# Whole-set loads of x, a later GpSimd subtraction and a spread seam in a fused set-attention and SwiGLU kernel

## The chip, the cores and the metric

The kernel runs on one NeuronCore of one Trainium2 chip. Five engines run side by side, each with its own queue of instructions in program order: PE (TensorE, matrix products; its weight loads are listed as PEld), DVE (VectorE), ACT (ScalarE), POOL (GpSimd) and SP (SyncE, which here issues nearly all DMAs). They meet only at semaphores. The metric is the device time of one execution in microseconds, as the median of several runs.

## The reference

Two blocks follow each other. The first is an induced set attention over x (4 batches of 12416 rows of 128 channels) with 32 inducing vectors; the second is a SwiGLU feed-forward network (FFN) with an RMS norm in front.

```python
def mab(q, kv):
    s = scale * (q @ kv.transpose(0, 2, 1))
    s = s - s.max(-1, keepdims=True)
    a = np.exp(s)
    a /= a.sum(-1, keepdims=True) + 1e-09
    return a @ kv
h = mab(I, x)          # 32 inducing rows look at 12416 rows of x
y = mab(x, h)          # every row of x looks at the 32 rows of h
...
rms = np.sqrt(np.mean(y * y, axis=-1, keepdims=True) + 1e-06)
yn = y / rms * rms_g
g = yn @ w_gate                     # 128 -> 1536
out = ((g / (1 + np.exp(-g))) * (yn @ w_val)) @ w_out    # 1536 -> 128
```

The second attention's row sum drops out under the RMS norm, so the kernel never divides by it. And since a row of y is a combination of 32 rows of h, the kernel multiplies h into w_gate and w_val once per batch, and the FFN's first products work on the 32 attention weights of a row instead of its 128 channels. The three weight matrices arrive as 64-bit floats and are turned into 32-bit ones on the chip.

## The kernel before

**Sets, units and slots.** A batch's 97 blocks of 128 rows are cut into 7 sets `s` (five of 16 blocks, one of 15, one of 2). For the FFN a set is cut into 4 quarters, the last one into 1: these are the 25 *units* `u` of a batch, of 512 rows as a rule. A unit passes through the 12 chunks `j` of d_ff, and one chunk of one unit is a *slot*; a batch has 300. A slot (`slot` in `ffn`) issues the gate product `g` on PE (L653), the silu on ACT (L661), then the output products that are due (`products`), the value product `v` on PE (L664), the product u = silu times v on DVE (L670), and at last `steps()`: everything that was planned for this slot. The first two units go through their slots in turns.

**The output product** of a chunk comes in two kinds. A plain one is one 32-bit product on PE (L603, `acc<-u,wo`, two rows in the profile) and is issued at the earliest two slots after its u. The *three-part* one (`three`, `project3`) replaces it by three cheaper PE products (L619, L621, and L603 in its form `acc<-xn,xn`). It needs, in the slot after its own, a copy on ACT (L640) and a subtraction on POOL (L641), and a slot later another copy on ACT (L645) and another subtraction on POOL (L646). The third PE product reads what L646 wrote.

**The order is written out in advance.** `schedule(b)` gives each attention step of a batch a slot number; the seams (below) have theirs in a table. Within `steps()` the waiting steps come first (the two halves of three-part products, a finished unit's output), then the plan, then the seams, then `gather`. A small planner (the loop that fills `ready`) walks over all slots with the costs of POOL's work, 1.25 us a slot, and chooses which chunks become three-part products and in which slot their PE products are due; `sub_max` counts 1.1 us in the slot where it is planned, a seam's `scale`, `apply` and `split` count 3.0, 1.2 and 1.4. It chooses 400 of the 1200 chunks.

**The prologue** (before the first slot) does the first batch's attention without cover. `load_rows` loads set after set of x on SP's queue: set 0 in three pieces, sets 1 and 5 in two, the others in one; set 6 goes in four small ones (L141). A weight chunk is fetched (`fetch_raw`) after set 2 and four more after set 6. For each set PE turns the blocks (`turn_x`, L322), ACT copies them out (L325), PE multiplies by the inducing vectors (`scores1`, L331) and DVE takes scores and maxima out (L335). `scores1` of a set comes after `turn_x` of the next one. DVE's work on the first weight chunk is put in between: `parts(0, 0)` (five instructions, L254 to L267 and L238) in the turn of set 3, `join(0, 0)` (L276, L282, then POOL's L284, a store and the next weight fetch) in that of set 4.

**Maxima.** `scores2(s)` writes the second attention's scores into the tile `sc` (L431); `sub_max(s)` takes each row's maximum on DVE (L436) and subtracts it on POOL (L437; for set 0 on DVE). Both are issued in one slot: in the first batch slot 2s+17, in the later ones, which are prepared under the batch before, slot 203+7s. ACT's exponential (`exp2`) follows from slot 30 and slot 254.

**Seams.** Between two sets, `seam(b, s)` makes the next set's FFN input in seven steps: `turn_a` (DVE, L499), `square` (PE, L505), `turn_z` (DVE, L512, L513), `scale` (DVE L517, L518, then a power on POOL, L520), `apply` (POOL, L524), `turn_b` (DVE, L528) and `split` (ACT L534, POOL L537). `gather` then brings a unit's rows together with four DMAs (L549); it is issued in chunk 2 of the unit before. The slots of the seven steps, counted from the first unit of the set before, stand in the line below: the first tuple for all seams but the first, the second for the first seam of batch 0.

```python
for i, step in enumerate(seam(*one)):
    j = ((14, 17, 18, 21, 21, 29, 31) if k else (32, 33, 33, 34, 34, 36, 38))[i]
    n, j = divmod(j, NJ)
    at = (b, firsts[s] + n + late_by, j)
```

## Time and profile before

| What | Value |
|---|---|
| median of 9 runs | 1673.86 us (1672.36 to 1675.46) |
| the profiled execution's own time | 1674.4 us |
| its span in the trace | 1672.6 us |
| mean granted TensorE clock | 0.998 |
| first FFN product (L653) starts at | 54.80 us |
| busy PE, ACT, DVE, POOL | 1654.5, 1237.0, 1175.5, 1160.3 us |
| DMA | 112.39 MB, mean 67 GB/s |

The 1200 slots take from 54.80 us to the end, 1.35 us each on the mean. Matmuls are pipelined and their ends are modelled: the idle time before a row, which the timeline gives in square brackets with what ended it, tells more than the busy time. A slot's place in time is found by its silu on ACT: the silus of slots 33, 38 and 48 start at 109.66, 116.00 and 132.77 us.

### The profile page before, as it was taken

The page shows a single profiled execution, that of the slowest core. Times are in us where ns is not written, and L with a number is a line of the kernel's source. Part 1 is how long each engine was busy: PE and PEld are TensorE (multiplying, and loading weights), DVE is VectorE, ACT ScalarE, POOL GpSimd, SP SyncE. Part 2 cuts the span into 40 slices and gives each one's busy share as a digit, 9 for nine tenths or more (in the row PEclk, how much of TensorE's full clock was granted, in tenths as well). Part 3 has the DMA queues.
Part 4 walks back from the last instruction along what each step waited for, and adds up shares of the span by engine and source line. Part 5 has one row for each costly group of instructions (what it writes and reads, how often), then busy time and mean ns, then how long its engine had stood idle before and what let it go on. Part 6 is the DMA issues. An engine that isn't in the chain of part 4 may idle for free.

```text
span 1672.6 us, 23254 instructions
## 1 busy us (share of the span) xinstructions
PE 1654.5 (99%) x6764; PEld 1036.4 (62%) x6764; DVE 1175.5 (70%) x1961; ACT 1237.0 (74%) x2234; POOL 1160.3 (69%) x931
## 2 busy tenths in 40 slices
PE   9999999999999999999999999999999999999998
PEld 6546566655676665665566666565567666666666
DVE  4878776676767877667677787667767666666665
ACT  4547778766787777776778777867677788788785
POOL 1337776767577775776578777577657888888884
PEclk9999999999999999999999999999999999999999
DMA  6445424343454131524345313252211111111111
GB/s 254 89 76 89 81 56 106 77 95 55 66 85 68 35 83 32 132 65 90 56 72 79 57 36 81 62 123 70 51 30 35 34 33 38 32 34 37 32 37 25
DMA packets 389743, 112.39 MB, mean 67 GB/s; under 512 B 365136, under 2 KB 369776, under 8 KB 387312
## 3 DMA queue, kind: packets, MB, share of 16 engines
q1 hardware_dynamic: 389424, 110.89, 32.6%
q8 instruction: 54, 0.88, 0.2%
q14 instruction: 73, 0.60, 0.1%
q10 hardware_dynamic: 192, 0.02, 0.0%
HBM read 53.95 MB, written 27.00 MB: 48 GB/s over the span
## 4 chain that ended last, share of the span: by engine, by line
PE 96%; DVE 1%; POOL 1%; DMA 1%; ACT 0%; issue 0%; SPq 0%; DVEq 0%; POOLq 0%
PE acc L603 45%; PE gv L653 17%; PE gv L664 16%; PE u L621 5%; PE u L619 5%; PE mm L331 3%; PE mm L505 1%; PE mm L384 1%; DMA xn<-in_x_dram 1%; DVE u L670 0%; POOL rs L520 0%; PE gv L322 0%; PE mm L457 0%; PE gv L331 0%; POOL xn L646 0%
## 5 line engine op out<-in xcount | busy, mean ns | idle before, releaser
L670 DVE TENSOR_TENSOR u<-silu,gv 128x512 f32<-128x512 f32 (+2 forms) x1186 | 779.8, 664 | 441.3 <-PE gv L664 227.5
L661 ACT ACTIVATE silu<-gv 128x512 f32<-128x512 f32 (+2 forms) x1186 | 691.8, 584 | 362.3 <-PE gv L653 326.8
L603 PE MATMUL acc<-u,wo 128*128 128x512 f32 (+2 forms) x1600 | 792.8, 579 | 1.2 <-DVE u L670 1.0
L664 PE MATMUL gv<-a,sv 128*128 128x512 f32 (+2 forms) x1188 | 759.8, 640 | 0.9 <-DVE u L670 0.9
L641 POOL TENSOR_TENSOR xn<-u,xn 128x512 fp32r<-128x512 f32 (+2 forms) x400 | 504.4, 1261 | 353.9 <-ACT xn L640 317.0
L646 POOL TENSOR_TENSOR xn<-hs,u 128x512 fp32r<-128x512 f32 (+2 forms) x400 | 504.4, 1261 | 39.6 <-ACT hs L645 36.6
L653 PE MATMUL gv<-a,sg 128*128 128x512 f32 (+2 forms) x1188 | 483.9, 407 | 0.0
L653 PEld LDWEIGHTS gv<-a,sg 128*128 128x128 f32 x1188 | 224.4, 189 | 228.9 <-ACT silu L661 110.9
L603 PEld LDWEIGHTS acc<-u,wo 128*128 128x128 f32 x1600 | 298.9, 189 | 77.9 <-issue 15.3
L664 PEld LDWEIGHTS gv<-a,sv 128*128 128x128 f32 x1188 | 224.3, 189 | 195.1 <-issue 135.9
L640 ACT ACTIVATE xn<-u 128x512 fp32r<-128x512 f32 (+2 forms) x400 | 247.7, 619 | 24.7 <-DVE u L670 22.8
L645 ACT ACTIVATE hs<-xn 128x512 f32<-128x512 f32 (+2 forms) x400 | 245.9, 615 | 5.6 <-POOL xn L646 4.2
L603 PE MATMUL acc<-xn,xn 128*128 128x512 f32 (+2 forms) x400 | 157.0, 392 | 4.5 <-POOL xn L646 4.5
L621 PE MATMUL u<-xn,xn 128*128 128x512 f32 (+2 forms) x400 | 155.6, 389 | 0.0
L619 PE MATMUL u<-xn,xn 128*128 128x512 f32 (+2 forms) x400 | 155.2, 388 | 0.0
L603 PEld LDWEIGHTS acc<-xn,xn 128*128 128x128 f32 x400 | 75.0, 188 | 25.1 <-POOL xn L646 8.6
L520 POOL TENSOR_TENSOR rs<-ms,mhalf 128x16 f32<-128x16 f32 (+2 forms) x28 | 75.9, 2711 | 16.5 <-DVE ms L518 14.7
L621 PEld LDWEIGHTS u<-xn,xn 128*128 128x128 f32 x400 | 75.1, 188 | 18.1
L619 PEld LDWEIGHTS u<-xn,xn 128*128 128x128 f32 x400 | 75.0, 188 | 16.9 <-issue 0.7
L612 DVE STREAM_TRANSPOSE o<-o 128x512 f32<-128x512 f32 (+2 forms) x97 | 67.7, 698 | 3.4
L611 DVE TENSOR_TENSOR o<-acc,o 128x512 f32<-128x512 f32 (+2 forms) x97 | 64.9, 669 | 0.0
L624 ACT ACTIVATE o<-u 128x512 f32<-128x512 f32 (+2 forms) x97 | 56.4, 582 | 0.0
(166 smaller groups left out, 774.0 us busy)
## 6 DMA issues: line engine op xcount, KB each, us to landing
out_dram<-o SPq DMA_DIRECT2D x320, 64.0 KB, 1.9
xn<-in_x_dram SPq DMA_DIRECT2D x62, 256.0 KB, 4.7
xT<-in_x_dram SPq DMA_DIRECT2D x60, 256.0 KB, 5.2
a<-hi SPq DMA_DIRECT2D x156, 64.0 KB, 2.0
a<-lo SPq DMA_DIRECT2D x156, 64.0 KB, 2.0
w<-w SPq DMA_DIRECT2D x22, 256.0 KB, 3.1
out_dram<-o SPq DMA_DIRECT2D x64, 60.0 KB, 1.9
xn<-in_x_dram SPq DMA_DIRECT2D x3, 1024.0 KB, 11.7
```

Of the source, the lines that this page charges most:

```text
L520: nc.gpsimd.tensor_tensor(out=rs, in0=ms, in1=mhalf[rows, 0:n], op=ALU.pow)
L603: nc.tensor.matmul(acc[:, 0:T], lhsT, rhs, start=st["left"] == NJ, stop=st["left"] == 1)
L619: nc.tensor.matmul(ups[:, 0:T], w[:, i, :], hi, start=st["k"] == nk, stop=False)
L621: nc.tensor.matmul(ups[:, 0:T], w[:, NK + i, :], lo, start=False, stop=not st["k"])
L640: nc.scalar.activation(hi, v, AF.Copy, scale=1.0 - 2.0 ** -13)
L641: nc.gpsimd.tensor_tensor(out=lo, in0=v, in1=hi.bitcast(F32), op=ALU.subtract)
L645: nc.scalar.activation(hs[:, 0:T], hi.bitcast(F32), AF.Copy, scale=1.0 + 2.0 ** -12)
L646: nc.gpsimd.tensor_tensor(out=d, in0=hs[:, 0:T], in1=v, op=ALU.subtract)
L653: nc.tensor.matmul(g[:, 0:T], sg[:, ts(j, P)], a[:, 0:T], start=True, stop=True)
L661: nc.scalar.activation(sl[:, 0:T], g[:, 0:T], AF.Silu)
L664: nc.tensor.matmul(v[:, 0:T], sv[:, ts(j, P)], a[:, 0:T], start=True, stop=True)
L670: nc.vector.tensor_tensor(out=t[:, 0:T], in0=sl[:, 0:T], in1=v[:, 0:T], op=ALU.mult)
```

## The change

There are three edits. x is loaded in whole sets but for set 0; with it the first `scores1` moves ahead of `turn_x(1)`, the first weight chunk is fetched after set 3 instead of set 2, and `parts` and `join` move one set later. `sub_max` is split: `row_max` (DVE) keeps the slot, the subtraction (POOL, or DVE for set 0) goes to the next one, and the planner counts it there. And in batch 0 the first seam's steps 2 to 6 go to slots 34, 35, 35, 39 and 41, with the gather behind them in chunk 6 of its unit instead of chunk 2. The lines that change:

```diff
-            for t0, t1 in (((0, R), (R, 2 * R), (2 * R, n)) if not s else ((0, 2 * R), (2 * R, n)) if s in (1, full - 1) else ((0, n),)):
+            for t0, t1 in (((0, R), (R, 2 * R), (2 * R, n)) if not s else ((0, n),)):
...
+        def row_max(s):
+            mx = st["mx2"] = small.tile([P, 16], F32, name="mx2")[rows2[s], 0:per2[s]]
+            nc.vector.reduce_max(out=mx, in_=weights(b, s), axis=AX.X)
+
         def sub_max(s):
-            n, v = per2[s], weights(b, s)
-            mx = small.tile([P, 16], F32, name="mx2")[rows2[s], 0:n]
-            nc.vector.reduce_max(out=mx, in_=v, axis=AX.X)
+            n, v, mx = per2[s], weights(b, s), st["mx2"]
             (nc.gpsimd if s else nc.vector).tensor_tensor(
...
-        for _ in range(1 if s == 2 else 4 if s == NS - 1 else 0):
+        for _ in range(1 if s == 3 else 4 if s == NS - 1 else 0):
...
-        if s:
-            f["scores1"](s - 1)
-        if s == 3:
+        if s != 1:
+            f["scores1"](max(s - 1, 0))
+        if s == 4:
             parts(0, 0, nc.vector)
-        if s == 4:
+        if s == 5:
             join(0, 0)
...
+    f["row_max"](0)
     f["sub_max"](0)
...
-                add(2 * s + 17, f["sub_max"], s)
+                add(2 * s + 17, f["row_max"], s)
+                add(2 * s + 18, f["sub_max"], s)
...
-                add(203 + 7 * s, g["sub_max"], s)
+                add(203 + 7 * s, g["row_max"], s)
+                add(204 + 7 * s, g["sub_max"], s)
...
-                j = ((14, 17, 18, 21, 21, 29, 31) if k else (32, 33, 33, 34, 34, 36, 38))[i]
+                j = ((14, 17, 18, 21, 21, 29, 31) if k else (32, 33, 34, 35, 35, 39, 41))[i]
...
-                if j == 2 and (b or u > 1) and (b, u) in after:
+                if j == (6 if (b, u) == (0, R - 1) else 2) and (b or u > 1) and (b, u) in after:
                     gather(*after[b, u])
```

## The prediction

> **What bounds the kernel now.** I read the page first. PE is busy nearly all the time and the chain that ended last runs through it:

> ```profile
> PE 1654.5 (99%) x6764; PEld 1036.4 (62%) x6764; DVE 1175.5 (70%) x1961; ACT 1237.0 (74%) x2234; POOL 1160.3 (69%) x931
> ...
> PE 96%; DVE 1%; POOL 1%; DMA 1%; ACT 0%; issue 0%; SPq 0%; DVEq 0%; POOLq 0%
> ```

> PE's work is the same after the change (1200 slots, 400 of them three-part), so only time in which PE waits or runs slowly can go. PE's waits come second:

> ```profile
> PE acc L603 <- POOL xn L646: 4.5, 4, 2.7
> ...
> PE mm L505 <- DVE eT L499: 0.6, 2, 0.4
> ```

> Behind the first slot POOL's L646 is the one releaser worth having: four waits, 4.5 us, one of 2.7. PE's timeline shows that one, in the first seam:

> ```profile
> 116.03 0.40 PE L621 MATMUL u<-xn,xn 128*128 128x512 f32 x1
> 119.12 0.74 PE L603 MATMUL acc<-xn,xn 128*128 128x512 f32 x1 [2.69 <-POOL xn L646]
> 119.65 0.63 PE L664 MATMUL gv<-a,sv 128*128 128x512 f32 x1
> ```

> The view by windows (PE's busy time comes second, the granted clock third from the end) adds that the clock drops right after:

> ```profile
> 116.50:119.20 2.70, 0.08 (x1) 0.09 (x1) 1.33 (x3) 1.17 (x3) 2.48 (x3) 1.00 0.00 0
> 119.20:122.70 3.50, 3.50 (x7) 2.09 (x8) 2.56 (x4) 0.63 (x2) 1.28 (x1) 0.51 0.21 53
> ```

> POOL's timeline tells why L646 is late: the power and the apply stand in front of it.

> ```profile
> 112.33 1.29 POOL L641 TENSOR_TENSOR xn<-u,xn 128x512 fp32r<-128x512 f32 x1 [7.81 <-ACT xn L640]
> 113.80 2.91 POOL L520 TENSOR_TENSOR rs<-ms,mhalf 128x16 f32<-128x16 f32 x1 [0.18 <-DVE ms L518]
> 116.78 1.05 POOL L524 TENSOR_TENSOR sc<-sc,rs 128x512 f32<-128x512 f32 x1
> 117.79 1.27 POOL L646 TENSOR_TENSOR xn<-hs,u 128x512 fp32r<-128x512 f32 x1
> ```

> The other three waits are one place, 405.7 us apart, where the subtraction L437 stands in front of L646 and itself waits 0.80 us for its maximum:

> ```profile
> 397.78 1.05 POOL L437 TENSOR_TENSOR sc<-sc,mx 128x512 f32<-128x512 f32 x1 [0.80 <-PE gv L653]
> 398.79 1.29 POOL L646 TENSOR_TENSOR xn<-hs,u 128x512 fp32r<-128x512 f32 x1
> ```

> Last the prologue, on DVE:

> ```profile
> 22.50 0.69 DVE L335 TENSOR_SCALAR_CACHE_REDUCE sc<-gv 128x512 f32<-128x512 f32 x1
> ...
> 23.72 0.69 DVE L282 SCALAR_TENSOR_TENSOR o<-sc,o 128x512 f32<-128x512 uint32 x1
> 25.29 0.69 DVE L335 TENSOR_SCALAR_CACHE_REDUCE sc<-gv 128x512 f32<-128x512 f32 x1 [0.88 <-PE gv L331]
> ...
> 26.60 0.66 DVE L335 TENSOR_SCALAR_CACHE_REDUCE sc<-gv 128x480 f32<-128x480 f32 x1 [0.61 <-PE gv L331]
> ```

> DVE has 0.88 and 0.61 us of slack there: that is what moved work can use up.

> **The first seam: -4.2 us.** With `scale` and `apply` a slot later, POOL's order becomes L641, L646, L520, L524: waiting steps come before seams. L641 ends at 113.62 and its copy L645 at 113.26, so L646 runs 113.6 to 114.9 instead of 117.79 to 119.07. PE has issued L621 at 116.03 and goes on at 116.27 (its rows lie 0.23 us apart elsewhere) instead of 119.12: 2.85 us. PE is then not idle, so the 3.41 us at half clock go too: half of them, 1.7 us. The window's sum is 4.55.

> What is late next? DVE: `turn_z` (L512, L513) moves behind slot 34's L670, `scale` behind slot 35's, so the power starts at about 115.1 instead of 113.80 and the apply ends at 119.15 instead of 117.84. `turn_b`, in slot 36, kept DVE idle for 2.74 us (L528 waiting for L524). In slot 39, with L670 (0.65 each) of slots 36 to 39, one L314 (0.69) and L611 and L612 (1.4) in front, DVE reaches it at about 119.65: no wait. In slots 39 to 43 DVE's L670 end just before PE wants them (slot 39's at 119.65, PE at 119.63); I allow 0.3 us for such waits, 0 to 1. The chunk of slot 38, newly three-part, is due in slot 44 (about 123.9); its L641 and L646 follow the apply and end at 121.8. -4.55 + 0.3 is about -4.2; bounds -4.6 (all of it) and 0 (another wait of the same size).

> The gather's four DMAs move on SP behind one xT load and unit 2's four stores, which go out earlier for it. L528 ends at 120.35, ACT's copy L534 is behind slot 41's silu (121.0), L537 waits for L646 and takes 1.28: 123.1. SP begins the stores when L612 is done, 119.3, and needs 3.37 us for them in this trace: 122.7; four issues of 0.6 bring the last to 124.5, and 2.0 from issue to landing (median of these DMAs) to 126.5. Unit 4's first product is wanted at 132.24 less 4.4, 127.8. Slack 1.3 us, cost 0; bounds 0 and, if they land as slowly as an xT load (5.2), 1.9.

> **The subtraction: -2.2 us.** In the first batch POOL has nothing between its six L437, so its order there, and the time, does not change; the exponential still stands behind the last. In later batches L646 of the preceding chunk now goes ahead of L437. At 397 it starts when L641 ends (396.98) and ends at 398.3; PE wants it at 399.36. The rows L621 to L603 lie 1.00 us apart there instead of 0.23: 0.77 in each of three places, 2.3; 0.1 is left for a later L641 behind the moved subtraction. The planner, by its own arithmetic, keeps its choice but for the chunk of slot 247, which becomes 245, in three batches. There the last subtraction (32x256, 0.61) does stand between L641 and L646. But its maximum is a slot old, so of 0.80 + 1.05 at the old place 0.61 are left: 1.24 less against a lateness of 0.77, so no wait. Bounds: -2.4, and 0 if each place only swaps one wait for another. Set 0's subtraction on DVE changes places with one L670, some 50 slots before its exponential: 0.

> **The prologue: +0.2 us.** DMA landings follow each other by bytes, 1 MB in 2.5 us (set 4's 18.97 after set 3's 16.47). The weight chunk (1.27 us) behind set 3 brings set 3 to 15.2, set 4 stays at 18.97, set 5 comes whole at 21.4 to 21.9. The three DMAs fewer save issue time that nothing waits for. `scores1(0)` needs ACT's fourth copy of set 0 (ends 10.12) and fills 10.15 to 11.2 while set 1 lands (10.0 to 10.2); `turn_x(1)` follows, then sets 2 (13.0) and 3 (15.9 instead of 16.61); set 4 waits for its load, 19.1 instead of 19.47. PE is 0.35 us ahead. DVE is not: L335 of set 3 at 22.1, `parts` 22.7 to 24.9 (2.14 in this trace), L335 of set 4 to 25.5, `join` (0.60 + 0.69) to 26.8, and only then L335 of set 5, 26.8 instead of 26.60. All that follows the maximum shifts by +0.2. `join`'s POOL product (1.27), its store and the fetch behind it come 2.4 us later: the weights are first used at 40.43, the fetched chunk at 58.39 (it landed at 30.81): 0. Bounds: -0.4 (PE's lead counts) and +1.0, as follows. In before PE turns blocks without a break from 7.58 to 11.4, and at 9.7 its rows begin to come at twice the pace. After the change it stands still from 9.4 to 10.15, and another 3.4 us at half pace (the one length this trace shows) would cost 1.7, of which the waits for loads hide 0.7.

> [...]

> **Sum.** -4.2 - 2.2 + 0.2 = -6.2 us. The profiled execution took 1674.4 (span 1672.6 and 1.8 around it) and becomes 1668.2; it lies 0.54 above the median, so the median becomes 1667.7, 0.37% less. About 0.2%, 3.3 us, is what a measurement of this kernel can tell from no change.

> **Rivals.**
> 1. *The seam's stall only moves* (7 in 100). PE waits as long elsewhere in slots 36 to 48, for u behind `turn_b` or for the gather. For it: DVE has no slack in slots 39 to 43. Against: no wait above 0.3 us comes out. -2.2 + 0.2 = -2.0: 1671.9, no measurable change.
> 2. *The subtractions only swap waits* (8 in 100). For it: slot 245 has the order that cost 0.77. Against: its maximum is there, and it is the short one. -4.2 + 0.2 = -4.0: 1669.9.
> 3. *The break in the prologue puts the full clock off* (10 in 100). -4.2 - 2.2 + 1.0 = -5.4: 1668.5.
> 4. *Slower* (5 in 100): in the three later batches L646 behind the moved subtraction comes so late that PE stands as in the first seam. Each such place costs 2.85 + 1.7 = 4.55 us; three make 13.7: 1674.4 - 4.2 + 0.2 + 13.7 - 0.5 = 1683.6. It turns the sign by 0.2% from 3.9 us a place on. Against: five slots (6.7 us) lie between chunk and product, and 0.63 + 1.29 + 0.61 + 1.29 = 3.8 must fit.

> **How the numbers follow.** The sum as worked has 70 in 100, its own range is 1666.0 to 1669.5 (the bounds -0.4 of the prologue and -4.6, -2.4 on one side, 1 us of DVE waits and 0.9 of a late gather on the other). Low 1665.8; high 1671.0 takes in rivals 2 and 3 and leaves out 1 and 4, 12 in 100, and some of the main case. Faster by over 0.2%: 83 (the sum, rivals 2 and 3, less 5 for both falling short together); within: 11; slower: 6.

> **What the profile will show.** Right: no PE wait for L646 (L648 there) near 116 to 119, a clock of 1.00 in 119 to 123; POOL's order L641, L646, power, apply; no idle time before `turn_b`; no wait at 399, 805 and 1211; L653 of slot 0 at about 55.0, with L335 of set 5 behind L282 without a gap. Wrong: a wait of unit 4 for its `a` near 128, a clock below 1.00 after 54 us, PE rows at half pace beyond 10 us, or a new wait for L648 near slot 250.

## The result and the profile after

The changed kernel takes **1667.34 us** (median of 9 runs, 1667.13 to 1669.1) beside 1673.92 us for the kernel before (29 runs, 1672.19 to 1675.46): 6.6 us less, a ratio of 0.9962 with a 95% interval of 0.9954 to 0.9971. The forecast was 1667.7. The profiled execution took 1667.41 us; its span is 1665.6 us, 7.0 less than the one shown of before. The two edits of the first seam and of the subtraction brought a little more than forecast, the edit of the loads cost a little more.

After the change every line below L437 stands two further down: L603, L646, L653, L664 and L670 are L605, L648, L655, L666 and L672, the seam's L499 to L537 are L501 to L539; the subtraction L437 is L439, the maximum L436 is L435. Among the experiments only the versions with `row_max` have the new numbers.

The page first. PE's busy time fell by 3.7 us with the same number of products (before, L653 took 0.63 us at 120.08, with 0.50 granted, beside 0.39 at 115.56, with 1.00; such rows behind the first seam are gone); its shares of the span and of the chain are as before, and POOL's 1% has left the chain.

```profile
PE 1650.8 (99%) x6764; PEld 1034.6 (62%) x6764; DVE 1174.9 (71%) x1961; ACT 1237.5 (74%) x2234; POOL 1160.0 (70%) x931
...
PE 96%; DVE 2%; DMA 1%; ACT 0%; issue 0%; POOL 0%; SPq 0%; DVEq 0%; POOLq 0%
```

PE's waits (us in all, number, longest). No line for `L605 <- POOL xn L648` is left; before, that was 4.5 us in four waits. What the prologue still has, and the wait for `turn_a` (L501), stay. Two larger waits in the prologue are new: the one for the maximum L340, and 0.73 us in front of the first L331 (at 9.69 us) for ACT's copy L325, the standstill that the prediction had put at 9.4 to 10.15.

```profile
PE acc L605 <- DVE u L672: 1.2, 3, 0.7
...
PE mm L507 <- DVE eT L501: 0.6, 2, 0.4
PE gv L344 <- DVE mx L340: 0.5, 1, 0.5
```

PE's timeline at the place of the old stall (start, duration): the third product of the three-part chunk follows the second after 0.23 us, where it stood 2.69 us before.

```profile
114.90 1.12 PE L605 MATMUL acc<-u,wo 128*128 128x512 f32 x2 [0.23 <-DVE u L672]
...
116.57 0.40 PE L623 MATMUL u<-xn,xn 128*128 128x512 f32 x1
116.80 0.39 PE L605 MATMUL acc<-xn,xn 128*128 128x512 f32 x1
```

The view by windows (PE, PEld, DVE, ACT, POOL busy, then granted clock, DMA share, GB/s): PE is full in both stretches, and the clock is 1.00 where it was 0.51.

```profile
115.50:119.00 3.50, 3.50 (x14) 2.38 (x13) 3.34 (x7) 2.31 (x4) 3.19 (x2) 1.00 0.00 0
119.00:122.50 3.50, 3.50 (x11) 1.82 (x11) 3.50 (x7) 2.83 (x5) 3.50 (x4) 1.00 0.29 50
```

POOL's timeline says why: L643 and L648 now run ahead of the power (L522) and the apply (L526). At 393 L648 runs ahead of the subtraction L439, which waits for nothing.

```profile
112.80 1.29 POOL L643 TENSOR_TENSOR xn<-u,xn 128x512 fp32r<-128x512 f32 x1 [7.81 <-ACT xn L642]
114.05 1.28 POOL L648 TENSOR_TENSOR xn<-hs,u 128x512 fp32r<-128x512 f32 x1
115.73 2.90 POOL L522 TENSOR_TENSOR rs<-ms,mhalf 128x16 f32<-128x16 f32 x1 [0.40 <-DVE ms L520]
118.71 1.05 POOL L526 TENSOR_TENSOR sc<-sc,rs 128x512 f32<-128x512 f32 x1
...
393.07 1.28 POOL L648 TENSOR_TENSOR xn<-hs,u 128x512 fp32r<-128x512 f32 x1
394.31 1.04 POOL L439 TENSOR_TENSOR sc<-sc,mx 128x512 f32<-128x512 f32 x1
```

PE's timeline shows what that is worth. Before, the third product of the chunk in front waited for L646:

```profile
399.13 0.40 PE L621 MATMUL u<-xn,xn 128*128 128x512 f32 x1
400.13 0.50 PE L603 MATMUL acc<-xn,xn 128*128 128x512 f32 x1 [0.60 <-POOL xn L646]
400.46 0.39 PE L664 MATMUL gv<-a,sv 128*128 128x512 f32 x1
```

After, the same three rows:

```profile
395.25 0.40 PE L623 MATMUL u<-xn,xn 128*128 128x512 f32 x1
395.48 0.40 PE L605 MATMUL acc<-xn,xn 128*128 128x512 f32 x1
395.71 0.40 PE L666 MATMUL gv<-a,sv 128*128 128x512 f32 x1
```

DVE's timeline, first in the prologue, then at `turn_b`: L335 of set 5 (26.88) follows `parts` and `join` without a gap, L254 behind it takes 0.80 us instead of 0.42, and `turn_b` (L530) waits for nothing.

```profile
25.05 0.69 DVE L335 TENSOR_SCALAR_CACHE_REDUCE sc<-gv 128x512 f32<-128x512 f32 x1
...
26.88 0.65 DVE L335 TENSOR_SCALAR_CACHE_REDUCE sc<-gv 128x480 f32<-128x480 f32 x1
...
27.79 0.80 DVE L254 TENSOR_SCALAR we<-sc 128x512 int32<-128x512 int32 x1
28.52 0.27 DVE L346 TENSOR_REDUCE row<-gv 1x32 f32<-1x128 f32 x1
...
120.09 0.69 DVE L530 STREAM_TRANSPOSE aT<-sc 128x512 f32<-128x512 f32 x1
```

Before, L254 and the L346 behind it stood so:

```profile
27.52 0.42 DVE L254 TENSOR_SCALAR we<-sc 128x512 int32<-128x512 int32 x1
28.06 0.28 DVE L346 TENSOR_REDUCE row<-gv 1x32 f32<-1x128 f32 x1
```

**Where the time went.** The silu of a slot marks the slot's place in time, so the difference of two profiles' silus of one slot says how far the one is ahead there. I call that the lead. After minus before:

| Slots | Lead, us | Step |
|---|---|---|
| 0 to 36 | +0.45 to +0.47 | prologue: +0.45 |
| 50 to 230 | -3.88 | first seam: -4.35 |
| 260 to 530 | -4.75 | subtraction, first place: -0.87 |
| 560 to 830 | -5.62 | second place: -0.87 |
| 860 to 1190 | -6.47 | third place: -0.85 |
| 1199 | -6.81 | last unit: -0.35 |
| end of the span | -7.0 | |

### The profile page after: what moved, and what is told of

It reads as the page before. It is cut to its first block, busy times and chain, and to the rows that moved or that the text cites. A ratio compares the mean times of both kernels' runs of the same rounds, so it can differ in the third digit from the quotient of the medians.

```text
span 1665.6 us, 23262 instructions
## 1 busy us (share of the span) xinstructions
PE 1650.8 (99%) x6764; PEld 1034.6 (62%) x6764; DVE 1174.9 (71%) x1961; ACT 1237.5 (74%) x2234; POOL 1160.0 (70%) x931
## 4 chain that ended last, share of the span: by engine, by line
PE 96%; DVE 2%; DMA 1%; ACT 0%; issue 0%; POOL 0%; SPq 0%; DVEq 0%; POOLq 0%
PE acc L605 45%; PE gv L655 17%; PE gv L666 16%; PE u L623 5%; PE u L621 5%; PE mm L331 3%; PE mm L507 1%; PE mm L384 1%; DMA xn<-in_x_dram 1%; DVE u L672 0%; PE mm L459 0%; PE mm L473 0%; DMA ind<-in_inducing_dram 0%; POOL rs L522 0%; PE gv L384 0%
## 5 line engine op out<-in xcount | busy, mean ns | idle before, releaser
L672 DVE TENSOR_TENSOR u<-silu,gv 128x512 f32<-128x512 f32 (+2 forms) x1186 | 779.8, 664 | 439.5 <-PE gv L666 226.7
L605 PE MATMUL acc<-u,wo 128*128 128x512 f32 (+2 forms) x1600 | 791.5, 579 | 1.2 <-DVE u L672 1.2
L666 PE MATMUL gv<-a,sv 128*128 128x512 f32 (+2 forms) x1188 | 757.8, 638 | 0.9 <-DVE u L672 0.9
L643 POOL TENSOR_TENSOR xn<-u,xn 128x512 fp32r<-128x512 f32 (+2 forms) x400 | 504.3, 1261 | 350.8 <-ACT xn L642 309.0
L648 POOL TENSOR_TENSOR xn<-hs,u 128x512 fp32r<-128x512 f32 (+2 forms) x400 | 504.2, 1261 | 40.3 <-ACT hs L647 36.9
L655 PE MATMUL gv<-a,sg 128*128 128x512 f32 (+2 forms) x1188 | 483.7, 407 | 0.0
L655 PEld LDWEIGHTS gv<-a,sg 128*128 128x128 f32 x1188 | 224.1, 189 | 227.9 <-ACT silu L663 110.1
L605 PEld LDWEIGHTS acc<-u,wo 128*128 128x128 f32 x1600 | 298.6, 188 | 78.8 <-issue 16.0
L666 PEld LDWEIGHTS gv<-a,sv 128*128 128x128 f32 x1188 | 224.0, 189 | 194.4 <-issue 133.5
L642 ACT ACTIVATE xn<-u 128x512 fp32r<-128x512 f32 (+2 forms) x400 | 247.7, 619 | 24.9 <-DVE u L672 22.8
L605 PE MATMUL acc<-xn,xn 128*128 128x512 f32 (+2 forms) x400 | 156.4, 391 | 0.0
L621 PE MATMUL u<-xn,xn 128*128 128x512 f32 (+2 forms) x400 | 155.2, 388 | 0.0
L522 POOL TENSOR_TENSOR rs<-ms,mhalf 128x16 f32<-128x16 f32 (+2 forms) x28 | 75.9, 2711 | 16.6 <-DVE ms L520 14.7
L605 PEld LDWEIGHTS acc<-xn,xn 128*128 128x128 f32 x400 | 75.0, 187 | 19.1 <-POOL xn L648 2.5
L621 PEld LDWEIGHTS u<-xn,xn 128*128 128x128 f32 x400 | 75.0, 188 | 16.9 <-issue 0.7
```

The source lines that it names most:

```text
L522: nc.gpsimd.tensor_tensor(out=rs, in0=ms, in1=mhalf[rows, 0:n], op=ALU.pow)
L605: nc.tensor.matmul(acc[:, 0:T], lhsT, rhs, start=st["left"] == NJ, stop=st["left"] == 1)
L621: nc.tensor.matmul(ups[:, 0:T], w[:, i, :], hi, start=st["k"] == nk, stop=False)
L642: nc.scalar.activation(hi, v, AF.Copy, scale=1.0 - 2.0 ** -13)
L643: nc.gpsimd.tensor_tensor(out=lo, in0=v, in1=hi.bitcast(F32), op=ALU.subtract)
L648: nc.gpsimd.tensor_tensor(out=d, in0=hs[:, 0:T], in1=v, op=ALU.subtract)
```

## The experiments

Eleven kernels ran, in three groups, each beside runs of the kernel before on its chip. All compute everything.

| Version | us, median (range, runs) | before there | ratio (95%) |
|---|---|---|---|
| loads_only | 1674.42 (1673.11 to 1675.43, 10) | 1674.21 | 1.0001 (0.9992 to 1.0011) |
| seam_only | 1669.83 (1669.44 to 1671.89, 10) | 1674.21 | 0.9976 (0.9967 to 0.9985) |
| sub_only | 1671.41 (1669.58 to 1671.74, 10) | 1674.21 | 0.9979 (0.9969 to 0.9989) |
| parts_back | 1666.77 (1666.73 to 1666.87, 4) | 1674.21 | 0.9956 (0.9941 to 0.9971) |
| pool_order_only | 1673.68 (1672.98 to 1675.13, 10) | 1674.21 | 1.0001 (0.9992 to 1.001) |
| turn_b_only | 1674.39 (1672.57 to 1676.44, 10) | 1674.21 | 1.0003 (0.9994 to 1.0012) |
| max_early | 1671.68 (1671.07 to 1673.31, 10) | 1674.21 | 0.9985 (0.9976 to 0.9994) |
| parts_back_turn_a | 1666.23 (1666.0 to 1667.49, 5) | 1674.21 | 0.9955 (0.9942 to 0.9969) |
| seam_sub | 1667.57 (1666.93 to 1668.9, 5) | 1674.11 | 0.9964 (0.9951 to 0.9978) |
| seam_sub_turn_a | 1666.80 (1666.39 to 1668.53, 5) | 1674.11 | 0.9962 (0.9949 to 0.9974) |
| all_again | 1667.89 (1667.3 to 1668.44, 5) | 1674.11 | 0.9965 (0.9953 to 0.9978) |

### One edit at a time

**loads_only** is the kernel before with the first edit alone:

```diff
-            for t0, t1 in (... ((0, 2 * R), (2 * R, n)) if s in (1, full - 1) else ((0, n),)):
+            for t0, t1 in (... ((0, n),)):
...
-        for _ in range(1 if s == 2 else 4 if s == NS - 1 else 0):
+        for _ in range(1 if s == 3 else 4 if s == NS - 1 else 0):
...
-        if s:
-            f["scores1"](s - 1)
-        if s == 3:
+        if s != 1:
+            f["scores1"](max(s - 1, 0))
+        if s == 4:
             parts(0, 0, nc.vector)
-        if s == 4:
+        if s == 5:
             join(0, 0)
```

> The first edit alone (loads of x, the first scores1, the weight fetch, parts and join). Theory (VectorE becomes the bound of the prologue): PE is ahead by 0.2 to 0.4 us when scores1 of set 5 ends, but L335 of set 5 starts behind L282 without a gap at about 26.9 instead of 26.60, and L254 behind it takes 0.8 instead of 0.42; the first FFN product starts at about 55.25 instead of 54.80, the whole takes 0.45 us more, 1674.3. The stall at 119 and the three at 400, 806 and 1211 stay. Rival (larger loads pay): the first FFN product at 54.4, 1673.5. Both lie within what the times can tell, so the trace decides.

Measured: 0.2 us more than before at the median, within what can be told. In the profiled execution the first FFN product came at 56.12 us (54.81 before) because the load of set 5 was late: it landed at 22.88 us (21.91 in the changed kernel's profile), and PE waited 1.17 us for it. At slots 36, 50, 400 and 1190 the lead is +1.30 to +1.35, so nothing changes behind the prologue; at slot 1199 it is +1.0. The DVE timeline shows the order that the change gives: L335 of set 5 without a gap behind `join`, and L254 at 0.80 us.

```profile
25.91 0.69 DVE L335 TENSOR_SCALAR_CACHE_REDUCE sc<-gv 128x512 f32<-128x512 f32 x1 [1.24 <-PE gv L331]
...
27.73 0.65 DVE L335 TENSOR_SCALAR_CACHE_REDUCE sc<-gv 128x480 f32<-128x480 f32 x1
...
28.64 0.80 DVE L254 TENSOR_SCALAR we<-sc 128x512 int32<-128x512 int32 x1
```

So no gain from this edit can be told; what can be told comes from the other two.

**seam_only** is the first seam's edit alone:

```diff
-  j = ((14, 17, 18, 21, 21, 29, 31) if k else (32, 33, 33, 34, 34, 36, 38))[i]
+  j = ((14, 17, 18, 21, 21, 29, 31) if k else (32, 33, 34, 35, 35, 39, 41))[i]
...
-  if j == 2 and (b or u > 1) and (b, u) in after:
+  if j == (6 if (b, u) == (0, R - 1) else 2) and (b or u > 1) and (b, u) in after:
```

> The first seam's slots and the gather's place alone. Theory: the stall near 116 to 119 and the half clock behind it go, nothing else moves: -4.3 us, 1669.6. Rival (the edits need each other, or the gather's place costs): -2.5 us or less, with a wait of PE for the unit's rows near 128.

Measured: 4.4 us less. Between slots 36 and 50 the lead changes by -4.35 us, the same as in the full change, and then stays. PE's waits keep the three for the subtraction:

```profile
PE acc L603 <- POOL xn L646: 1.8, 3, 0.6
```

**sub_only** is the split of maximum and subtraction alone:

```diff
+        def row_max(s):
+            mx = st["mx2"] = small.tile([P, 16], F32, name="mx2")[rows2[s], 0:per2[s]]
+            nc.vector.reduce_max(out=mx, in_=weights(b, s), axis=AX.X)
...
-                add(2 * s + 17, f["sub_max"], s)
+                add(2 * s + 17, f["row_max"], s)
+                add(2 * s + 18, f["sub_max"], s)
...
-                add(203 + 7 * s, g["sub_max"], s)
+                add(203 + 7 * s, g["row_max"], s)
+                add(204 + 7 * s, g["sub_max"], s)
```

> The split of sub_max alone, with the planner's new choice of one chunk a batch. Theory: the waits of 0.60 us for L646 at 400, 806 and 1211 go, 0.77 to 0.87 us each: -2.3 to -2.6 us, 1671.4; the first batch is unchanged to the slot. Rival (the waits only swap places, or the chunk of slot 245 waits): 0 to -1 us, with a new wait for L648 near slot 250.

Measured: 2.8 us less, and the lead grows at the same three places (by 0.85, 0.87 and 0.89 us). The one long wait stays. PE's timeline:

```profile
115.30 0.40 PE L623 MATMUL u<-xn,xn 128*128 128x512 f32 x1
118.38 0.50 PE L605 MATMUL acc<-xn,xn 128*128 128x512 f32 x1 [2.68 <-POOL xn L648]
...
119.64 1.25 PE L666 MATMUL gv<-a,sv 128*128 128x512 f32 x1
```

The last row takes 1.25 us where its like at 123.93 us takes 0.79; the clock record has half clock from 119.82 us, 1.4 us after the wait had ended (118.38). That looked odd, and is taken up below. The three medians add up to 0.2 - 4.4 - 2.8 = -7.0 us beside -6.6 measured for all together, and the lead makes the same steps alone and together: the edits don't hide each other.

**parts_back** is the changed kernel with `parts` and `join` in the turns of the kernel before; loads, seam and subtraction stay changed:

```diff
-        if s == 4:
+        if s == 3:
             parts(0, 0, nc.vector)
-        if s == 5:
+        if s == 4:
             join(0, 0)
```

> The changed kernel, but parts and join of the first weight chunk go back by one set (the chunk lands at 16.65 us, before scores1 of set 2 is through on VectorE). Theory (VectorE's late work and its meeting with GpSimd's product made the prologue longer): L335 of set 5 starts at 26.4 instead of 26.88, the L254 behind the maximum takes 0.42 instead of 0.80, the first FFN product starts at about 54.5 instead of 55.26: 0.7 us less than the changed kernel, 1666.6. Rival (the loads, or PE's break before 9.7 us, are what costs): 55.2 stays, 1667.3.

Measured: 1666.77 us, 0.57 below the changed kernel. The two were not timed in one group, and the intervals of their ratios overlap, so the size is open; the place is in the DVE timeline: the idle time before set 5's L335 is back and L254 takes 0.42 us.

```profile
26.58 0.66 DVE L335 TENSOR_SCALAR_CACHE_REDUCE sc<-gv 128x480 f32<-128x480 f32 x1 [0.61 <-PE gv L331]
...
27.50 0.42 DVE L254 TENSOR_SCALAR we<-sc 128x512 int32<-128x512 int32 x1
28.04 0.28 DVE L346 TENSOR_REDUCE row<-gv 1x32 f32<-1x128 f32 x1
```

### The two halves of the seam's edit

The prediction said that the order on POOL makes the gain, and that `turn_b` would be late next. The two runs take one half each.

**pool_order_only**: `turn_z` to `apply` a slot later, `turn_b`, `split` and the gather where they were.

```diff
-  j = ((14, 17, 18, 21, 21, 29, 31) if k else (32, 33, 33, 34, 34, 36, 38))[i]
+  j = ((14, 17, 18, 21, 21, 29, 31) if k else (32, 33, 34, 35, 35, 36, 38))[i]
```

> The kernel before with scale and apply a slot later (slots 32, 33, 34, 35, 35, 36, 38), turn_b, split and gather where they were. GpSimd's order is then mended (L646 before the power), VectorE's turn_b is still only a slot behind apply. Theory (two waits lie on top of each other, and one edit alone moves the stall): PE does not wait for L646, but L528 waits for the apply, which ends at 119.2, some 2.9 us, slot 37's u comes at about 120.4, and PE waits for it 1.5 to 2.5 us at slots 39 to 40; the clock may halve as before. 0 to -2.5 us, 1672 to 1674. Rival (GpSimd's order is all): -4.3 us, 1669.6.

**turn_b_only**: the other half.

```diff
-  j = ((14, 17, 18, 21, 21, 29, 31) if k else (32, 33, 33, 34, 34, 36, 38))[i]
+  j = ((14, 17, 18, 21, 21, 29, 31) if k else (32, 33, 33, 34, 34, 39, 41))[i]
...
-  if j == 2 and (b or u > 1) and (b, u) in after:
+  if j == (6 if (b, u) == (0, R - 1) else 2) and (b or u > 1) and (b, u) in after:
```

> The other half: slots 32, 33, 33, 34, 34, 39, 41 and the gather in chunk 6, scale and apply where they were. Theory: the wait of 2.74 us on VectorE goes, but L646 stays behind the power and the apply; PE waits 2.7 us at 119 and runs at half clock for 3.41 us behind it: 0 to -0.5 us, 1673.7. Rival (VectorE's wait is what counted): -4.3 us, 1669.6.

Measured: 1673.68 and 1674.39 us, both no change. With the POOL order alone PE passes the old place without a wait and stands 2.61 us in the next slot, for a u that L670 delivers late, because in DVE's queue L528 (`turn_b`) stands in front of it and waits 3.55 us for the apply. PE's timeline:

```profile
118.45 0.39 PE L603 MATMUL acc<-xn,xn 128*128 128x512 f32 x1
...
122.79 0.49 PE L664 MATMUL gv<-a,sv 128*128 128x512 f32 x1 [2.61 <-DVE u L670]
```

and DVE's:

```profile
121.45 0.71 DVE L528 STREAM_TRANSPOSE aT<-sc 128x512 f32<-128x512 f32 x1 [3.55 <-POOL sc L524]
```

With `turn_b` moved alone the old wait stands unchanged:

```profile
119.05 0.80 PE L603 MATMUL acc<-xn,xn 128*128 128x512 f32 x1 [2.67 <-POOL xn L646]
```

Each half alone gives nothing, both together 4.4 us. Rival 1 of the prediction ("the seam's stall only moves") is what happens with one half; the edit escapes it by moving both.

### Is it the order, or the wait for the maximum?

**max_early** leaves each subtraction in its slot and takes the maximum a slot earlier:

```diff
+        def row_max(s):
+            mx = st["mx2"] = small.tile([P, 16], F32, name="mx2")[rows2[s], 0:per2[s]]
+            nc.vector.reduce_max(out=mx, in_=weights(b, s), axis=AX.X)
...
+                add(2 * s + 17, f["row_max"], s)
                 add(2 * s + 17, f["sub_max"], s)
...
+                add(202 + 7 * s, g["row_max"], s)
                 add(203 + 7 * s, g["sub_max"], s)
```

> The kernel before with the maximum a slot earlier in the three later batches (slot 202+7s), the subtraction where it was: GpSimd's order and the planner's choice are as before, but L437 no longer waits for its maximum. Theory (lateness is a sum: 0.80 waiting plus 1.05 of work in front of L646, of which 0.77 are too much): L437 starts at 396.98 after L641, L646 ends at 399.3, PE wants it at 399.36: the three waits go, -2.2 us, 1671.7. Rival (the order is what counts): the waits stay at 0.5 us or more, 1673.5.

Measured: 2.5 us less, by steps of 0.82 us at the same three places. POOL's timeline shows the order of before, without the 0.80 us in front of the subtraction:

```profile
396.78 1.30 POOL L643 TENSOR_TENSOR xn<-u,xn 128x512 fp32r<-128x512 f32 x1
398.02 1.06 POOL L439 TENSOR_TENSOR sc<-sc,mx 128x512 f32<-128x512 f32 x1
399.03 1.30 POOL L648 TENSOR_TENSOR xn<-hs,u 128x512 fp32r<-128x512 f32 x1
```

PE's product that needs this L648 starts at 400.45, 0.24 us after the row in front of it, where 0.23 is usual; L648 had just ended (399.03 + 1.30 = 400.33). So the order alone was not the fault. The 0.80 us for which the subtraction waited in POOL's queue was enough to make L646 late, and either remedy removes nearly all of it (0.82 us a place here, 0.85 to 0.87 in the changed kernel).

### A better version, and what the loads are worth

What PE still waited for at the seam was `turn_a` (L501, 0.40 us). **parts_back_turn_a** is parts_back with that step a slot earlier:

```diff
-  j = (... if k else (32, 33, 34, 35, 35, 39, 41))[i]
+  j = (... if k else (31, 33, 34, 35, 35, 39, 41))[i]
```

> The changed kernel with parts and join a set earlier (as in parts_back) and the first seam's turn_a in slot 31 instead of 32. The exponential of set 1 ends at about 106, so eT can be made behind slot 31's u, at about 108, and the square in slot 33 does not wait. Theory: the wait of 0.40 us for eT at 110.2 goes, 0.4 to 0.9 us: 1666.1, 0.6 below parts_back and 1.2 below the changed kernel. Rival (VectorE and the table load bound these slots, so PE waits for a later u instead): 1666.8.

Measured: **1666.23 us**, the lowest median of all versions, 8.0 us below before. Between slots 33 and 36 the kernel gains 0.6 us (the same in seam_sub_turn_a below), and the seam's wait is gone from PE's list (the 0.2 is another place):

```profile
PE mm L507 <- DVE eT L501: 0.2, 1, 0.2
```

Is the loads edit needed at all? **seam_sub** is the changed kernel with the first edit undone (the diff of loads_only, reversed), **seam_sub_turn_a** the same with step 31 for 32, and **all_again** the changed kernel once more beside them.

> The change without its first edit: loads, parts and join as before, seam and subtraction as in the change. Theory A (the whole-set loads cost the changed kernel time, because parts and join moved a set later): about 0.5 us faster than the changed kernel, so 1666.8 us, as the version with parts and join moved back (1666.77), with the first seam and the subtractions saving 4.4 + 2.8 = 7.2 us of 1674.0. Theory B (the loads edit pays in the company of the other two): slower than the changed kernel, 1667.5 to 1668.5 us. In the profile: no wait of PE for L648, POOL's order L643, L648, power, apply, the first FFN product within 0.8 us of 54.8.

> The same with the seam's first step a slot earlier (31 in place of 32). Theory A: the wait of PE's L507 for L501 (0.40 us) goes, so 0.5 us below the run before, about 1666.3 us, level with the version that has whole-set loads with parts and join moved back and this step (1666.23). Theory B: 1667.0 to 1668.0 us. In the profile: no wait of 0.4 us at PE's L507 near 110.

> The changed kernel once more, on the same chip as the two versions without its first edit: 1667.3 us, as measured (1667.34), from 0.3 to 0.8 us above the version without the first edit by theory A and below it by theory B.

Measured: 1667.57, 1666.80 and 1667.89 us. Without the edit the kernel is 0.3 us below the changed one on the same chip, with ranges that overlap: by theory A it should have been some 0.5 less, by theory B more, and neither is shown. Behind the prologue the two profiles agree: the lead moves by -6.95 us from slot 36 to slot 1199 in seam_sub and by -6.93 us from slot 36 to slot 1190 in the changed kernel. Whether whole loads with `parts` and `join` at their old places (1666.23) beat the loads in pieces (1666.80) is open too.

The reason is in the prologue's own spread. The first FFN product starts at 54.81, 54.48, 54.05, 56.05, 54.73, 55.87, 56.02 and 54.61 us in the eight profiles with loads in pieces, at 55.26, 56.12 and 55.50 in the three with the whole edit, and at 54.80 and 54.83 in the two with `parts` and `join` back. The same prologue code spreads over 2.0 us, and in the late ones PE's waits for the loads of x are the larger ones (4.3 us in seam_sub against 1.1 in before, which has the same prologue). The last piece of set 5 lands between 20.95 us (sub_only) and 23.02 (seam_sub), a spread of the same size; whole, it lands between 21.91 and 22.88, so no gain or loss of the load itself shows. A price of 0.2 to 0.5 us can't be told from that by medians of 5 to 10 runs. One part of it the profiles do tell: from the start of set 5's L335 to the first FFN product it takes 28.38 or 28.39 us in the three profiles with the whole edit, and 28.20 to 28.22 in the ten others. These 0.18 us are the longer L254, and parts_back, which has whole loads, is free of them.

## Why the prediction was right, point by point

- **First seam, -4.2 us: measured -4.35**, in the full change and alone. The order on POOL came as worked out, each start later by the prologue's 0.47: L648 at 114.05 (said 113.6), the power at 115.73 (115.1), the apply's end at 119.76 (119.15), `turn_b` at 120.09 (119.65) without a wait. Of the 0.3 us allowed for waits of DVE in slots 39 to 43, one of 0.23 came, but in slot 37. The 1.7 us for the half clock stands in the profile of before; whether a run of before holds it too differs from one execution to the next, by what the runs of sub_only show further down.
- **The gather, 0: right**, with less slack than said. Its last DMA landed at 127.26 us and unit 4's first product starts at about 128.2: 0.95 us instead of 1.3.
- **Subtraction, -2.2 us: measured -2.58**; the term was 0.4 too small. The three places gave 0.87, 0.87 and 0.85 where the working had 0.77 each less 0.1 in all. The rest is the row behind the wait: before, it stands 0.33 us after the product that waited (400.13 to 400.46), after the change 0.23 (395.48 to 395.71), which makes 0.87 a place; and the 0.1 set aside for a later L641 wasn't needed. And nothing had to be paid back: the lead that slot 256 showed for a moment (-5.36) was level again at slot 260. That rival 2 fails is shown by the empty list of waits for L648; max_early shows the mechanism from the other side.
- **Prologue, +0.2 us: measured +0.45 in the profiled execution**, +0.69 in all_again and +1.31 in loads_only, against a profile of before whose own prologue spreads by 2.0 us; only 0.18 of it is told apart from that spread. The step named came as named: L335 of set 5 at 26.88, without a gap (26.8 said). Of the 0.46 us by which L346 comes later, 0.28 are this. The other 0.18 the prediction didn't have: because `join` was moved a set later, its POOL product L284 (27.05 to 28.32) now runs when DVE comes to the power step's L254, and that L254 takes 0.80 us instead of 0.42. parts_back moves L284 away and has neither. The prediction priced the move of L284 itself at 0.
- **Rival 3, a later full clock: not seen.** The clock record says full from 7.29 us in the profile after, from 9.98 in the one before; over the other runs it is 4.5 to 10.1 with no pattern by version. In the profile after, PE's 0.73 us of standstill (up to 9.69) come when the record already says full, and it says so until 1662.75. That a break of this size is followed by 3.4 us more at half pace, which the +1.0 rests on, no run shows: it was my estimate.
- **Rival 4, slower by a late L648: not seen**; no such wait is left anywhere.
- **Not in the forecast: -0.35 us in the last unit.** Five of five profiles with the whole-load edit have a step of 0.73 or 0.74 us between two silus of the last unit (slots 1196 and 1197) where all eight without it have 1.08 to 1.11. In the profile before, an L670 at 1662.28 starts 0.40 us after the last release that the trace shows for it; its neighbours start 0.06 after. What delays it was not found; that the edit causes it is only a pattern of the runs.

Sum: +0.45 - 4.35 - 2.58 - 0.35 = -6.8 us in the profiles, and 0.2 more behind the last slot, beside -6.2 forecast. The median moved by 6.6. The terms missed by -0.15 (seam), -0.4 (subtraction) and +0.25 us (prologue), and -0.35 stood in no term; that the total came within 0.6 us of the profiles' sum owes something to their opposite signs. One sum in the prediction is off as well: its bounds of -0.4, -4.6 and -2.4 give 1666.5 us as the low end of its own range, not 1666.0, and its range counts 0.9 us for a late gather where its working has 1.9.

## What to carry to other kernels

When an in-order engine is not the bound, look for instructions in its queue that wait or run long directly in front of one that the bound engine needs: taking 0.80 us of waiting away in front of L646 paid 0.82 us at each of three places, and so did taking the power out of its way. Then ask who stands behind the moved step in its *other* queues before moving it: POOL's reorder and DVE's `turn_b` gave nothing singly and 4.4 us together. And a step of off-path work that seemed free (`join`) met a later instruction of another engine: with its L284 running, L254 took 0.80 us instead of 0.42. Check what runs beside such a step at its new place.

## What the runs showed of the hardware

| Version | idle in the stall's fullest window, us | next window |
|---|---|---|
| before | 2.69 | half clock |
| max_early | 2.69 | half clock |
| turn_b_only | 2.63 | half clock |
| loads_only | 2.39 | half clock |
| sub_only | 1.98 | half clock |
| pool_order_only | 1.78 | full clock |

The last run had nearly the same stall (2.61 us), but the grid cut it in two: PE is idle for 0.83 us in one window and for 1.78 in the next. The view by windows of max_early, whose second line is the grid window of the stall:

```profile
116.80:120.20 3.40, 0.71 (x5) 0.23 (x3) 1.26 (x3) 1.60 (x3) 3.26 (x3) 1.00 0.00 0
120.20:123.60 3.40, 3.40 (x6) 2.08 (x7) 2.64 (x5) 0.70 (x2) 1.28 (x1) 0.50 0.17 43
```

and of pool_order_only, cut at its grid:

```profile
117.60:121.00 3.40, 2.57 (x10) 1.43 (x8) 0.29 (x1) 1.09 (x2) 3.32 (x2) 1.00 0.00 0
121.00:124.40 3.40, 1.61 (x5) 1.05 (x6) 2.95 (x5) 1.72 (x3) 1.70 (x2) 1.00 0.08 19
124.40:127.80 3.40, 3.40 (x11) 1.81 (x11) 3.37 (x7) 1.33 (x3) 0.00 (x0) 1.00 0.31 71
```

sub_only's odd delay fits: the record went to half clock at the end of the grid window (119.82 us), 1.4 us after the stall. And the 1.7 us of the forecast seem to be there in some executions and not in others: sub_only, which keeps the stall (2.68 us in its profile), has 7 of 10 times at 1671.0 to 1671.7 (mean clocks 0.998 and 0.999) and 3 at 1669.6 to 1669.8 (1.000). If the boundary lay near 1.9 us, between the rows of 1.98 and 1.78, a 2.69 us stall at a random phase would pass it in (3.41 - 2.69 + 2 x 0.79) / 3.41 = 0.67 of the executions, an estimate from these rows and the 3.413 us alone. It is a rough one, because idle time by itself does not tell these cases apart. In pool_order_only 1.43 us of idle time around 54 us were followed by half clock, while the same 1.43 in other profiles was not; 1.61 us in parts_back's grid window up to 1661.16 were, and 1.80 us in the first full-clock window of seam_sub (4.49 to 7.91) were not. What else counts was not shown. The kernel before fits but proves little: its 52 runs of the first two groups have mean clocks of 0.999 (16 runs, median 1672.61 us), 0.998 (22, 1674.23) and 0.997 (14, 1675.26), which is one group more than one window makes, and the mean also holds the half clock at the kernel's end (from 1668.86 us in the profile before).

**L254 and L267 beside POOL's L284.** A DVE TENSOR_SCALAR of 128x512 (L254, L267) that takes 0.42 us with POOL idle (L254 at 27.52 in the profile before) took 0.80 to 0.92 us where POOL's product L284 was already running, and ended 0.27 to 0.29 us after it: in the profile after at 28.59 with L284's end at 28.32, in loads_only at 29.44 with 29.16. In the profile before there are three more such rows (L254 at 43.81, 0.90 us, L267 at 59.32 and 70.07, 0.91 each). Where the DVE instruction was first it was the other way round: there L254 at 58.39 kept its 0.42 us, and L284, from 58.55, took 1.39 instead of 1.27. So the introduction's "only at semaphores" says too much: the long DVE rows have no idle time in front that a semaphore ended, and yet took 0.80 to 0.92 us. What holds them up was not shown. The two POOL rows of the changed kernel and of parts_back:

```profile
27.05 1.27 POOL L284 TENSOR_TENSOR w<-o,we 128x512 f32<-128x512 f32 x1 [24.52 <-DVE o L282]
```

```profile
23.69 1.28 POOL L284 TENSOR_TENSOR w<-o,we 128x512 f32<-128x512 f32 x1 [21.18 <-DVE o L282]
```

Not every POOL instruction went with a longer row: in the profile before two TENSOR_SCALARs of this size took 0.43 us (at 49.49) and 0.42 (at 49.83) while the power L520 (47.62, 3.29 us) was running.
